# w_in in two tiles, PSUM banks 2 and 2, and both scores of a pair in one visit: an attention and MLP kernel on one core

## The chip, the cores and the metric

The kernel runs on one core of one Trainium2 chip. The metric is the device time of one execution in microseconds (us). Times are medians and ranges of all executions; ratios use fast executions alone (one counts as slow when it is over 1.5% above the fastest of the same kernel). A "span" is the time from the first to the last instruction of the one execution that was profiled, and is 1 to 2 us shorter than that execution's time.

Engines are named as the profile names them: PE is TensorE, PEld its weight loads, DVE VectorE, ACT ScalarE, POOL GpSimd. "Clock" is the share of full speed that was granted to PE.

## The reference

Eight batches of eight heads of attention over 576 positions (four heads with a local mask of 32 positions, four with a strided mask), whose output goes through two layers of an MLP. There are 4608 rows in all; the output is float32.

```python
scores = scale * np.matmul(q, k.transpose(0, 1, 3, 2))        # 8 x 8 heads, 576 x 576, head width 64
masks = [mask_local if h < 4 else mask_strided for h in range(8)]
attn = softmax(where(masks, scores, -1e9))
x = (attn @ v) as 4608 x 512
h = x @ w_in                                                   # 512 x 2048
g = np.where(h > 0.0, h, np.exp(np.minimum(h, 0.0)) - 1.0)
return g @ w_out                                               # 2048 x 512
```

## The kernel before

The masks leave so few positions that attention is cheap. Each batch is handled in eight pieces, four head pairs by two halves: transposes of q and k (T), scores (S), exp on ACT (e), times a 0/1 mask on DVE (pm), then matmuls that give the outputs and their sums (M), and a tail (E): ln and exp on ACT (ln, rc) give the reciprocal of the sums, and DVE multiplies into xT. Layer 1 takes 256 rows of xT and 256 columns of w_in in a group of eight matmuls (hps; a wide form of sixteen is hpw), layer 2 takes quarters of four matmuls into a tile of 128 rows (ops), which ACT copies out (osb).

The results of matmuls land in PSUM. The kernel uses eight banks of it: four for attention and wide groups (two tiles of two banks), three for layer 1, one for layer 2:

```python
p_x = tile_pool(name="ps_x", bufs=2)      # tiles of two banks: scores, wide groups
p_h = tile_pool(name="ps_h", bufs=3)      # layer 1; narrow transposes; s_ps and o_ps of batch 0
p_o = tile_pool(name="ps_o", bufs=1)      # layer 2; at the start, a scratch tile for spins
...
w_in_sb = const([128, KC, d_ff], BF16, "w_in_sb")      # one tile, loaded in two halves
```

Batch 0 is attention alone, with "spins" (matmuls on a constant, whose result nobody reads, f below) put between to keep the clock up:

```python
for it in ("f7 S0 S1 f6 T1 f6 S2 S3 m f10 T2 f6 S4 S5 f3 X3 f3 S6 f3 S7 M4 f3 E4 M5 f3 E5 M6 f3 E6 "
           "v M7 f3 E7 M0 f3 E0 M1 f3 E1 M2 f3 E2 M3 f10 E3").split():
```

T2 is the transposes of pair 2, X3 those of pair 3 (T3q and T3k, in the change, its q and its k apart), p sets the memsets of padding rows, m builds the strided mask, v casts v. The memsets that give constant columns (ones) and zeroed padding rows are on POOL, after this loop:

```python
nc.gpsimd.memset(qs[64:RP], 0.0)          # padding rows, 1.80 us each
nc.gpsimd.memset(ks[64:RP], 0.0)
...
nc.gpsimd.memset(qlb[64:RP], 0.0)
...
for i in range(2):                        # ones beside v: four memsets, 0.74 to 1.23 us each
    for t, n in ((vlx[i], LB), (vsx[i], NS)):
        nc.gpsimd.memset(t...[:, :, 1, :], 1.0)
```

After a second stage (batch 1, first layer-2 tiles) the main loop alternates groups of layer 1 with quarters of layer 2 and starts pieces of attention at set points between them; before the change the two scores of a head pair are half a group apart, so PE goes to attention twice.

The softmax here doesn't subtract the row's maximum and nothing guards it: scores larger than these inputs give would overflow.

## Time and profile before

| | before |
|---|---|
| time, median of 3 | 344.11 us (342.29 to 346.48) |
| span, mean clock | 343.4 us, 0.99 |
| PE, DVE, ACT, POOL busy | 320.0, 241.6, 220.9, 110.3 us |
| last xT of batch 0 ends | 27.37 us |
| first and second matmul of layer 1 | 26.14 and 29.57 us |
| main loop (128 groups of layer 1): start of the fifth, the 107th, the 125th | 81.55, 295.74, 327.00 us |

PE at 93% busy is the bound, and the prediction shows the lines for it. In excerpts in the order of time the columns are start us, us, engine, line, operation, out<-in, shape, count, and in brackets the idle time before it and what ended it.

### The profile page before, as it was taken

The numbers are of one execution on the slowest core, as the hardware profiler recorded it, in microseconds if no ns is written. First come the engines' busy times: TensorE is split into PE (matmuls) and PEld (weight loads), VectorE is DVE, ScalarE is ACT, GpSimd is POOL, SyncE is SP. The second block draws the span as 40 slices with busy tenths as digits, with TensorE's granted clock in tenths as the row PEclk, the third lists the DMA queues.
The fourth block names the chain that finished last, engine by engine and source line by source line (L and its number), as shares of the span: only waits on it lengthen the run. The fifth ranks groups of instructions, "written<-read, shape, count | busy, mean of one in ns | idle before, by whom it ended". The sixth has DMA issues, their size and how long they took to land.

```text
span 343.4 us, 7671 instructions
## 1 busy us (share of the span) xinstructions
PE 320.0 (93%) x2967; PEld 221.7 (65%) x2967; DVE 241.6 (70%) x476; ACT 220.9 (64%) x427; POOL 110.3 (32%) x129
## 2 busy tenths in 40 slices
PE   8686998877999999999999999999999999999995
PEld 6554864456666666676676666666777666777762
DVE  4541994337677788788888887789888776766660
ACT  3483667648667777677787766777777767444441
POOL 8068654830176260727006361545000000000000
PEclk9998999989999999999999999999999999999999
DMA  8999999999269944995169948992191101111211
GB/s 160 185 197 197 222 183 134 122 177 182 43 119 166 201 123 92 158 209 149 31 124 181 201 105 145 208 187 77 43 171 52 32 29 35 32 32 31 52 41 61
DMA packets 55179, 41.98 MB, mean 122 GB/s; under 512 B 38296, under 2 KB 45784, under 8 KB 55144
## 3 DMA queue, kind: packets, MB, share of 16 engines
q0 software_dynamic: 21040, 24.49, 43.5%
q1 hardware_dynamic: 32780, 16.42, 22.7%
q10 hardware_dynamic: 1324, 0.59, 1.0%
q8 instruction: 23, 0.38, 0.5%
q14 instruction: 12, 0.10, 0.1%
HBM read 38.18 MB, written 9.44 MB: 139 GB/s over the span
## 4 chain that ended last, share of the span: by engine, by line
PE 65%; ACT 11%; DMA 10%; DVE 8%; issue 3%; POOL 2%; SPq 0%; ACTq 0%; DVEq 0%
PE ops L451 30%; PE hps L392 27%; DMA w_in_sb<-in_moe_w_in_dram 6%; PE sc L283 3%; ACT osb L456 3%; ACT he L400 2%; DVE g L408 2%; DVE he L407 2%; DMA out_dram<-osb 2%; ACT ln L339 2%; ACT ln L338 2%; PE ox L335 1%; DMA ksT<-ks 1%; DVE g L428 1%; PE tp L258 1%
## 5 line engine op out<-in xcount | busy, mean ns | idle before, releaser
L451 PE MATMUL ops<-w_out_sb,g 128*128 128x512 bf16 x576 | 147.1, 380 | 3.7 <-ACT osb L456 3.5
L392 PE MATMUL hps<-xT,w_in_sb 128*128 128x256 bf16 x1088 | 143.4, 276 | 2.5 <-DVE xT L307 1.8
L392 PEld LDWEIGHTS <-w_in_sb 128*128 128x128 bf16 x1088 | 116.5, 114 | 23.1 <-issue 2.9
L400 ACT ACTIVATE he<-hps 128x512 f32<-128x512 f32 x136 | 80.6, 594 | 63.9 <-PE hps L392 61.8
L408 DVE TENSOR_TENSOR g<-he,hps 128x512 bf16<-128x512 bf16 x130 | 89.3, 687 | 13.9 <-DVE he L407 0.5
L451 PEld LDWEIGHTS <-g 128*128 128x128 bf16 x576 | 52.0, 98 | 44.4 <-issue 5.5
L407 DVE TENSOR_SCALAR he<-he 128x512 bf16<-128x512 f32 x130 | 63.1, 485 | 24.4 <-ACT he L400 23.3
L286 ACT ACTIVATE e<-sc 128x576 bf16<-128x576 f32 (+1 forms) x64 | 40.7, 645 | 14.5 <-PE sc L283 14.5
L456 ACT COPY osb<-ops 128x512 f32<-128x512 f32 x36 | 21.0, 582 | 11.7 <-PE ops L451 11.0
L307 DVE TENSOR_TENSOR xT<-ox,rc 64x288 bf16<-64x288 f32 x40 | 18.2, 454 | 7.3 <-ACT rc L341 6.5
L303 DVE TENSOR_TENSOR xT<-ox,rc 64x288 bf16<-64x288 f32 x40 | 18.1, 454 | 6.3 <-ACT rc L341 5.7
L129 POOL DMA_DIRECT2D qs<-in_q_dram x8 | 6.3, 792 | 39.6 <-DMA qsT<-qs 32.9
L338 ACT ACTIVATE ln<-ox 64x288 f32<-64x288 f32 x40 | 16.3, 407 | 4.1 <-PE ox L335 3.1
L341 ACT ACTIVATE rc<-ln 128x288 f32<-128x288 f32 x40 | 17.8, 444 | 1.3
L288 DVE TENSOR_TENSOR pm<-e,mask_s 72x576 bf16<-72x576 bf16 x32 | 15.2, 492 | 4.2 <-ACT e L286 4.1
L150 POOL COPY vsx<-vs 72x1024 bf16<-72x1024 bf16 x10 | 10.5, 1073 | 21.4 <-DMA vs<-in_v_dram 21.4
L294 DVE TENSOR_TENSOR pm<-e,mask_l 128x576 bf16<-128x576 bf16 x32 | 14.7, 473 | 3.7 <-ACT e L286 3.4
L138 POOL CAST klb<-kl 96x768 bf16<-96x768 f32 x11 | 10.7, 994 | 18.1 <-DMA kl<-in_k_dram 10.7
L144 POOL CAST vlx<-vl 128x768 bf16<-128x768 f32 x13 | 11.2, 889 | 16.1 <-DMA vl<-in_v_dram 13.6
L339 ACT ACTIVATE ln<-ox 64x288 f32<-64x288 f32 x40 | 16.1, 403 | 0.5
L461 PE MATMUL idle<-warm 128*128 128x256 bf16 x83 | 14.4, 315 | 1.3 <-DVE warm L173 1.3
L283 PEld LDWEIGHTS <-ksT 64*128 64x128 bf16 x256 | 5.9, 98 | 11.8 <-issue 7.7
(95 smaller groups left out, 268.8 us busy)
## 6 DMA issues: line engine op xcount, KB each, us to landing
out_dram<-osb SPq DMA_DIRECT2D x32, 144.0 KB
vl<-in_v_dram POOLq DMA_DIRECT2D x7, 576.0 KB, 17.2
kl<-in_k_dram POOLq DMA_DIRECT2D x6, 576.0 KB, 13.9
ql<-in_q_dram POOLq DMA_DIRECT2D x5, 576.0 KB, 14.8
qs<-in_q_dram POOLq DMA_DIRECT2D x8, 288.0 KB, 7.1
ks<-in_k_dram POOLq DMA_DIRECT2D x8, 288.0 KB, 8.8
vs<-in_v_dram POOLq DMA_DIRECT2D x8, 288.0 KB, 9.6
w_in_sb<-in_moe_w_in_dram POOLq DMA_DIRECT2D x2, 1024.0 KB, 19.5
```

The source lines that it names most:

```text
L286: nc.scalar.activation(e[0:R], sc[0:R, :, 0:W], ACT.Exp, scale=scale)
L303: nc.vector.tensor_mul(xs[:, u * W:(u + 1) * W], o[pr], rc[pr])
L307: nc.vector.tensor_mul(dst, o[pr].rearrange(pat, b=3, s=NS), rc[pr].rearrange(pat, b=3, s=NS))
L338: nc.scalar.activation(ln[lo], o[0][hi], ACT.Ln)
L339: nc.scalar.activation(ln[hi], o[1][lo], ACT.Ln)
L341: nc.scalar.activation(rc, ln, ACT.Exp, scale=-1.0)
L392: nc.tensor.matmul(hps[:, mm], lhsT=w_in_sb[:, c, (m // 4) * 512:(m // 4 + 1) * 512].rearrange("c (p mm) -> c mm p", mm=4)[:, m % 4], rhs= ...
L400: nc.scalar.activation(e, hps, ACT.Exp)
L407: eng.tensor_scalar(e1, e, scalar1=1.0, scalar2=1.0, op0=ALU.min, op1=ALU.subtract)
L408: nc.vector.tensor_tensor(gt, e1, hps, op=ALU.max)
L451: nc.tensor.matmul(ops, lhsT=g[:, m, kk * 128:(kk + 1) * 128], rhs=w_out_sb[:, m, :], start=(m == 0), stop=(m == MC - 1))
L456: nc.scalar.copy(o_sb, ops)
```

## The change

Its intent: layer 1's first columns need only the first half of w_in, so two tiles let them start when that half is in; two banks for layer 2 take away its wait for ACT's copy; one visit to the scores instead of two saves PE a switch. To get layer 1 started earlier it also reorders batch 0: the spins write free columns of live banks instead of a bank of their own, a cast moves from ACT to DVE, and the memsets move ahead. The core of the diff:

```diff
-    p_h = ctx.enter_context(tc.tile_pool(name="ps_h", bufs=3, ...))
-    p_o = ctx.enter_context(tc.tile_pool(name="ps_o", bufs=1, ...))
+    p_h = ctx.enter_context(tc.tile_pool(name="ps_h", bufs=2, ...))
+    p_o = ctx.enter_context(tc.tile_pool(name="ps_o", bufs=2, ...))
...
-    w_in_sb = const([128, KC, d_ff], BF16, "w_in_sb")
+    w_in_sb = [const([128, KC, d_ff // 2], BF16, f"w_in_sb{i}") for i in range(2)]
... piece_S: spins from here on go into the scores' bank
+        idle[0] = sc[:, 1, W:512]
... mm_O2, batch 0: s_ps in a layer-2 bank, spins from here on beside it
+            s_ps, idle[0] = ss[:, 0:W], ss[:, W:512]
... the start
-    idle = p_o.tile([128, 256], F32, tag="o", name="idle")
+    first = p_x.tile([128, 256], F32, tag="x", name="idle")
+    idle = [first]
...
+    for i in range(2):
+        for t, n in ((vlx[i], LB), (vsx[i], NS)):
+            nc.gpsimd.memset(t...[:, :, 1, :], 1.0)
-    for it in ("f7 S0 S1 f6 T1 f6 S2 S3 m f10 T2 f6 S4 S5 f3 X3 f3 S6 f3 S7 M4 f3 E4 ...
-               "v M7 f3 E7 M0 f3 E0 M1 f3 E1 M2 f3 E2 M3 f10 E3").split():
+    for it in ("f7 S0 S1 f6 T1 f6 S2 S3 m f8 T2 T3q S4 S5 T3k p f3 S6 S7 M4 f3 E4 ...
+               "v M7 f3 E7 M0 f3 E0 M1 f3 E1 M2 f3 E2 M3 f12 E3").split():
...
+        elif it == "p":
+            for t in (qlb, qs, ks):
+                nc.gpsimd.memset(t[64:RP], 0.0)
         elif it == "v":
-            cast_v(nc.scalar, 0, 0)
+            cast_v(nc.vector, 0, 0)
... (the old memsets after the loop are gone, with them a short one that zeroed rows of vlx)
... (the order of the second stage is new too, and layer 2 now takes all its tiles from p_o)
... second stage: the last narrow group of each tile in a layer-2 bank
-            l1(j, 4 * h + 3)
+            l1(j, 4 * h + 3, bank="o")
... main loop
-                at(SC[b][i] + .5 * u, lambda ...: do(("S", b, p, u)))
+                at(SC[b][i] + (.5 * u if b == 2 else 0), lambda ...: do(("S", b, p, u)))
```

More of the change, by code (lines that the diff above doesn't have):

```diff
@@ L58 @@
     p_x = ctx.enter_context(tc.tile_pool(name="ps_x", bufs=2, space=bass.MemoryType.PSUM))
-    p_h = ctx.enter_context(tc.tile_pool(name="ps_h", bufs=3, space=bass.MemoryType.PSUM))
-    p_o = ctx.enter_context(tc.tile_pool(name="ps_o", bufs=1, space=bass.MemoryType.PSUM))
+    p_h = ctx.enter_context(tc.tile_pool(name="ps_h", bufs=2, space=bass.MemoryType.PSUM))
+    p_o = ctx.enter_context(tc.tile_pool(name="ps_o", bufs=2, space=bass.MemoryType.PSUM))
     ctx.enter_context(tc.manual_schedule())
@@ L191 @@
     for i in range(2):
-        nc.gpsimd.dma_start(out=w_in_sb[:, :, i * 1024:(i + 1) * 1024],
+        nc.gpsimd.dma_start(out=w_in_sb[i],
                             in_=w_in_v[:, :, i * 1024:(i + 1) * 1024])
@@ L248, in piece_T @@
         else:
-            ps = [p_h.tile([128, S], BF16, tag="h", name="tp") for _ in range(2)]
+            ps = [p_h.tile([128, S], BF16, tag="h", name="tp"),
+                  p_o.tile([128, S], BF16, tag="o", name="tp")]
         for i, (dst, blk) in enumerate(both):
@@ L260, in piece_T, with piece_S @@
             copy(engs[i] if engs else nc.vector, dst, ps[i])
-    def piece_S(b, hp, u, fill=0):
+    def piece_S(b, hp, u):
         i_, a, st, pb = b % 2, hp % 2, hp >= 2, pitch(b)
@@ L266, in piece_S @@
         R = RS if st else 128
-        for _ in range(fill):
-            spin(sc[:, 1, W:W + 224])
+        idle[0] = sc[:, 1, W:512]
         for i in range(4 if st else 3):
@@ L350, in mm_O2 @@
         else:
-            s_ps = p_h.tile([128, W], F32, tag="h", name="s_ps")
+            ss = p_o.tile([128, 512], F32, tag="o", name="s_ps") if pool is None else p_h.tile(
+                [128, 512], F32, tag="h", name="s_ps")
             o_ps = p_h.tile([128, W], F32, tag="h", name="o_ps")
+            s_ps, idle[0] = ss[:, 0:W], ss[:, W:512]
         R = RS if hp >= 2 else 128
@@ L381, with w_in_of, l1 @@
     g_of = {}
-    def l1(j, t, mode="A"):
+    def w_in_of(m, c):
+        w = w_in_sb[m // (MC // 2)][:, c].rearrange("c (j p mm) -> c j mm p", mm=4, p=128)
+        return w[:, m // 4 % 2, m % 4]
+    def l1(j, t, mode="A", bank="h"):
         if t == 0:
@@ L386, in l1 @@
         g = g_of[j]
-        hps = p_h.tile([128, 2, SUB], F32, tag="h", name="hps")
+        hps = (p_h if bank == "h" else p_o).tile([128, 2, SUB], F32, tag=bank, name="hps")
         r0 = (j * SUB) % RING
@@ L393, in l1 @@
                     hps[:, mm],
-                    lhsT=w_in_sb[:, c, (m // 4) * 512:(m // 4 + 1) * 512].rearrange(
-                        "c (p mm) -> c mm p", mm=4)[:, m % 4],
+                    lhsT=w_in_of(m, c),
                     rhs=xT[:, c, r0:r0 + SUB],
@@ L419, in l1_wide @@
                     hps[:, mm],
-                    lhsT=w_in_sb[:, c, t * 256:t * 256 + 512].rearrange(
-                        "c (p mm) -> c mm p", mm=4)[:, mm],
+                    lhsT=w_in_of(2 * t + mm, c),
                     rhs=xT[:, c, r0:r0 + SUB],
@@ L482, in do @@
             tail_O2(*it[1:4], mm_O2(*it[1:4], pms.pop(it[1:4]), p_x))
-    idle = p_o.tile([128, 256], F32, tag="o", name="idle")
+    first = p_x.tile([128, 256], F32, tag="x", name="idle")
+    idle = [first]
     def spins(n):
         for _ in range(n):
-            spin(idle)
+            spin(idle[0])
     spins(26)
@@ L498 @@
     P = [(p, u) for p in range(4) for u in range(2)]
-    for it in ("f7 S0 S1 f6 T1 f6 S2 S3 m f10 T2 f6 S4 S5 f3 X3 f3 S6 f3 S7 M4 f3 E4 M5 f3 E5 M6 f3 E6 "
-               "v M7 f3 E7 M0 f3 E0 M1 f3 E1 M2 f3 E2 M3 f10 E3").split():
-        n = int(it[1]) if len(it) > 1 else 0
+    for i in range(2):
+        for t, n in ((vlx[i], LB), (vsx[i], NS)):
+            nc.gpsimd.memset(t.rearrange("p a t (y d) -> p (a t) y d", d=D)[:, :, 1, :], 1.0)
+    for it in ("f7 S0 S1 f6 T1 f6 S2 S3 m f8 T2 T3q S4 S5 T3k p f3 S6 S7 M4 f3 E4 M5 f3 E5 M6 f3 E6 "
+               "v M7 f3 E7 M0 f3 E0 M1 f3 E1 M2 f3 E2 M3 f12 E3").split():
+        n = int(it[1:].strip("qk")) if len(it) > 1 else 0
         if it == "m":
@@ L505 @@
             spins(n)
+        elif it == "p":
+            for t in (qlb, qs, ks):
+                nc.gpsimd.memset(t[64:RP], 0.0)
         elif it == "v":
-            cast_v(nc.scalar, 0, 0)
+            cast_v(nc.vector, 0, 0)
             cast_v(nc.gpsimd, 0, 1)
-        elif it[0] in "TX":
-            piece_T(0, n, (nc.vector, nc.scalar if n > 1 else nc.vector), it[0] == "X")
+        elif it[0] == "T" and len(it) == 3:
+            dst, blk = t_parts(0, n, it[2])
+            pool, tag = (p_h, "h") if it[2] == "q" else (p_o, "o")
+            ps = pool.tile([128, S], BF16, tag=tag, name="tp")
+            for j, x in enumerate(blk):
+                nc.tensor.transpose(ps[:, j * RS:(j + 1) * RS], x, identity[0:RS, 0:RS])
+            copy(nc.vector, dst, ps)
+        elif it[0] == "T":
+            piece_T(0, n, (nc.vector, nc.scalar if n > 1 else nc.vector), False)
         elif it[0] == "S":
@@ L513 @@
         elif it[0] == "M":
-            do(("M", 0, *P[n], p_h))
+            do(("M", 0, *P[n], None))
         else:
@@ L525, in spreads @@
             spread_v(nc.gpsimd, b, a)
-    nc.gpsimd.memset(qs[64:RP], 0.0)
-    nc.gpsimd.memset(ks[64:RP], 0.0)
     load_str(1, qs, q)
@@ L539 @@
     load_wo(3)
-    nc.gpsimd.memset(qlb[64:RP], 0.0)
     load_kl(1, nc.gpsimd)
@@ L543 @@
     load_vl(1, nc.gpsimd)
-    for i in range(2):
-        for t, n in ((vlx[i], LB), (vsx[i], NS)):
-            nc.gpsimd.memset(t.rearrange("p a t (y d) -> p (a t) y d", d=D)[:, :, 1, :], 1.0)
-    nc.gpsimd.memset(vlx[0][0:PRE, :, 0].rearrange("p a (y d) -> p a y d", d=D)[:, :, 0:3:2, :], 0.0)
     for h in range(2):
@@ L568, in l2_to @@
             j, kk, part = L2S[l2n[0]]
-            h = kk and (j == 0 or l2n[0] >= n_late)
-            l2(j, kk, part, *((p_h, "h") if h else (p_o, "o")))
+            l2(j, kk, part, p_o, "o")
             l2n[0] += 1
-    n_late = len(L2S)
-    for it in ("2 S4 2 S5 2 2 X4 2 S6 X5 2 S7 2 X6 2 X7 v "
-               "a 2 T0 2 S0 S1 2 T1 k B0 2 E0 S2 2 B1 S3 E1 2 B2 E2 2 B3 t 2 E3 x").split():
+    for it in ("2 S4 2 S5 2 B4 2 S6 E4 2 A5 S7 E5 2 B6 E6 2 A7 E7 v "
+               "a 2 T0 2 S0 S1 2 T1 k B0 2 E0 S2 2 A1 E1 S3 2 B2 E2 2 A3 t 2 2 E3 x").split():
         n = int(it[-1]) if it[-1].isdigit() else 0
@@ L634 @@
             for u in range(2):
-                at(SC[b][i] + .5 * u, lambda b=b, p=p, u=u: do(("S", b, p, u)))
+                at(SC[b][i] + (.5 * u if b == 2 else 0), lambda b=b, p=p, u=u: do(("S", b, p, u)))
                 at(SC[b][i] + 1.5 + .5 * u,
@@ L646 @@
             f()
-        l1(j, t, mode="B" if n < 18 and n % 3 == 0 else "A")
-    n_late = l2n[0]
+        l1(j, t, mode="B" if n < 18 and n % 3 == 0 else "A",
+           bank="o" if n in (2, 3) else "h")
     l2_to(len(L2S))
```

## The prediction

> **What bounds the kernel now.** I read the page first, then five-microsecond windows, then the order of time at the places where PE stops.
>
> ```profile
> PE 320.0 (93%) x2967; PEld 221.7 (65%) x2967; DVE 241.6 (70%) x476; ACT 220.9 (64%) x427; POOL 110.3 (32%) x129
> ...
> L451 PE MATMUL ops<-w_out_sb,g 128*128 128x512 bf16 x576 | 147.1, 380 | 3.7 <-ACT osb L456 3.5
> L392 PE MATMUL hps<-xT,w_in_sb 128*128 128x256 bf16 x1088 | 143.4, 276 | 2.5 <-DVE xT L307 1.8
> ...
> L400 ACT ACTIVATE he<-hps 128x512 f32<-128x512 f32 x136 | 80.6, 594 | 63.9 <-PE hps L392 61.8
> L408 DVE TENSOR_TENSOR g<-he,hps 128x512 bf16<-128x512 bf16 x130 | 89.3, 687 | 13.9 <-DVE he L407 0.5
> ```
>
> PE is the bound: ACT waits for layer 1 (61.8 us) while PE waits 3.5 us for ACT. Busy time alone does not show PE's pace, so I took the time from one start to the next: an eight-matmul layer-1 group holds PE for 0.88 us, a layer-2 quarter for 0.87. From about 106 us on PE hardly stops. The two soft places are in the start-up (windows: PE, PEld, DVE, ACT and POOL busy, granted clock, DMA):
>
> ```profile
> 30.00:35.00 5.00, 5.00 (x33) 3.94 (x32) 0.60 (x1) 2.57 (x4) 3.56 (x4) 0.66 1.11 212
> ...
> 75.00:80.00 5.00, 4.28 (x43) 3.06 (x43) 2.43 (x5) 3.27 (x6) 0.00 (x0) 0.70 1.03 173
> ```
>
> Both follow an idle PE and run at half clock for 3.5 us. The order of time around the first:
>
> ```profile
> 29.57 2.82 PE L418 MATMUL hpw<-xT,w_in_sb 128*128 128x256 bf16 x15 [3.15 <-DMA w_in_sb<-in_moe_w_in_dram]
> ...
> 34.40 1.22 DVE L428 SCALAR_TENSOR_TENSOR g<-we,wr 128x1024 bf16<-128x1024 f32 x1 [7.03 <-ACT wr L427]
> ...
> 36.67 2.37 DVE L407 TENSOR_SCALAR he<-he 128x512 bf16<-128x512 f32 x1
> ...
> 48.62 1.04 PE L451 MATMUL ops<-w_out_sb,g 128*128 128x512 bf16 x4
> ```
>
> The first matmul of layer 1 went at 26.14, the second waited for w_in to 29.56. The halves were issued at 6.9 and 7.7 us and took 17.2 and 21.8, so they landed at 24.1 and 29.5: the wait is for the half that these columns do not need. The attention of batch 0 gave its last xT at 27.38. From 34.40 to 51.77 DVE is the bound.
>
> **What the Trainium skill says.** "PSUM — Partial Sum Buffer", section "PSUM bank collisions raise a hardware error": two engines may not touch one bank and partition quadrant at once, even in disjoint columns. Here the trace agrees that order is forced: ACT's copy of one half of a transpose tile waits for DVE's copy of the other (2.1 us in two places). "SBUF — State Buffer", "Who interferes with whom": a DVE cast or tensor-scalar in a two-port mode and a GpSimd instruction block each other; the 2.37 us at L407 (0.43 otherwise) lie under four POOL memsets, which agrees. "TensorEngine Tiling (Array Packing)", "Key Properties": a change of tiling mode drains TensorE; below I measure about 0.1 us on each side of a visit to the scores. "TensorE: Matmul & The Clock Gate", "What's actually happening": half clock after an idle window of about 3.4 us. Here idle stretches of 3.3 and 2.0 us gave it, ones of 1.1 to 1.2 did not.
>
> **Part 1, w_in in two tiles, and the new start.** If batch 0 finished as before, layer 1 would start at 27.4 instead of 29.56 and at full clock: 2.1 + about 1.5. But the spinning matmuls now write free columns of a live bank. After scores they wait for the exp; before a logarithm (ln) of the same bank, ln waits for them. In the second half a pair needs: its output matmuls plus three spins 0.7, ln 0.42, rc 0.44, xT 0.51, then the output bank is free for the pair after next: about 2.15 us per two, or 1.08 each, where ACT now sets 0.79. Eight pieces: 8.6 against 8 x 0.79 + 0.81 (the ACT cast that moves to DVE) = 7.1. Twelve spins ahead of the last ln add 0.8. The scores of pieces 6 and 7 start as before (about 18.5), so I get a last xT near 29.2. The memsets of ones now lie at 9 to 12 us, over the k cast of 9.79 us: I add about 1 us. Layer 1 starts at 30.3, not 29.56, but warm (saves 1.5): DVE's first g comes at 30.3 + 1.75 + 2.05 = 34.1. The memsets gone from 36.7 save 1.9 on DVE, so its last g of this stretch ends near 34.1 + 17.4 - 1.9 = 49.6 instead of 51.77.
>
> Against that: the fourth of the narrow layer-1 groups now borrows a layer-2 bank. Layer 2 begins with both row halves of the first tile, so its second quarter (48.62 before) must wait for that last g. PE stands for some 3 us, long enough for half clock: 49.6 + (two quarters and a score, 2.1) + 1.7 = 53.4 for the point that was reached at 52.2 + 0.9 = 53.1. Later a transpose waits for another's copies (+0.75), and a wait for osb of 0.6 goes. The gap before 74.3 us stays: osb, ln, rc and xT still follow the last quarter. Start-up in sum: +0.4.
>
> **Part 2, banks 3 and 1 to 2 and 2.** Every second layer-2 tile waited for ACT's copy of the one before. From 85 to 334 us I summed every hold of PE over 0.12 us (start to start, less the columns' own time) that the trace puts down to osb: 10, in all 4.94 us. These go. But layer 1 now may run only two groups ahead. For each group I set the end of its last DVE read against the start of the group two later; where the read ends later, PE will have to wait. The usual evacuation takes 1.9 us and leaves 0.5 to 1.5. Around attention outputs ACT falls behind:
>
> ```profile
> 214.01 0.45 ACT L341 ACTIVATE rc<-ln 128x288 f32<-128x288 f32 x1
> 214.36 0.56 ACT L456 COPY osb<-ops 128x512 f32<-128x512 f32 x1
> 214.95 0.41 ACT L338 ACTIVATE ln<-ox 64x288 f32<-64x288 f32 x1
> ...
> 216.15 0.58 ACT L400 ACTIVATE he<-hps 128x512 f32<-128x512 f32 x1
> ```
>
> ```profile
> 217.77 0.69 DVE L408 TENSOR_TENSOR g<-he,hps 128x512 bf16<-128x512 bf16 x1
> ```
>
> ```profile
> 213.70 1.04 PE L392 MATMUL hps<-xT,w_in_sb 128*128 128x256 bf16 x8
> 214.97 1.02 PE L451 MATMUL ops<-w_out_sb,g 128*128 128x512 bf16 x4 [0.23 <-ACT osb L456]
> 215.83 1.04 PE L392 MATMUL hps<-xT,w_in_sb 128*128 128x256 bf16 x8
> 216.71 1.03 PE L451 MATMUL ops<-w_out_sb,g 128*128 128x512 bf16 x4
> 217.57 1.04 PE L392 MATMUL hps<-xT,w_in_sb 128*128 128x256 bf16 x8
> ```
>
> The group of 213.70 is read until 218.46; the group two later started at 217.57 (216.30 + 0.87 = 217.17 without the osb hold). It must now start at 218.5: a hold of 1.35 in place of 0.40. The same subtraction, with the lost osb hold and 0.06 for the wake-up added and consecutive overlaps counted once, gives for the four pairs of each batch: batch 3: 1.0, 0.9, 0.9, 1.35; 4: 1.1, 1.3, 0.4, 0.9; 5: 0.15, 1.15, 0.1, 1.35; 6: 1.1, 0.4, 0.05, 0.85; 7: 0.05, 0.85, 0.1, 1.35. Sum 15.4. Net of 4.94: +10.4. After the last output every group leaves 0.55, so the tail is free.
>
> **Part 3, both scores in one visit.** Between 106 and 290 us a visit of eight or six score matmuls costs 0.333 us from start to start, of which 0.10 is entry, 0.11 the matmuls, 0.13 the exit. Two visits cost 0.67, one double visit about 0.46: 0.2 us x 20 pairs = -4.1.
>
> Sum: 344.1 + 0.4 + 10.4 - 4.1 = 350.8. I take 350.0, since whoever made the change probably saw some gain that I miss.
>
> **Rivals.** First, the holds of part 2 come out small, because the scores moved forward relieve ACT and DVE just there. For it: ACT is busy only 64%. Against it: at 214 to 216 the queue holds two tails and an osb and no score. With half the holds: 342 to 343. Second, the spins do not hold ln back and the memsets hit nothing: layer 1 starts near 26.5, warm, 4 to 5 us earlier. For it: the ACT cast really goes. Against it: the bank rule. This makes 346 to 347. Third, the stand before the second layer-2 quarter is worse, with both half-clock stretches: 353 to 355.
>
> **Range and chances.** Start-up is uncertain by 3 us either way, the holds by 4, the visits by 1: together about 5, hence 343 to 356. 2% slower begins at 351.0, just above my centre: 0.42; within 2%: 0.50. Faster by 2% (337.2) needs both the first and the second rival: 0.08.
>
> **What would show it.** Waits of layer 1 (PE hps or its weight load) for DVE g, about 10 to 15 us in all, 0.7 before; waits of ops for osb gone; 20 fewer entries into scores; the first L418 run near 30 us at full clock; a PE gap near 47 to 49 us ended by DVE g, with half clock after it. I am wrong if layer 1 starts before 28 us, or if holds for g stay under 5 us.

## More of the kernel before

```profile
7.48 0.37 DVE L204 COPY mask_l<-base_l 128x576 bf16<-128x576 bf16 x1
...
11.87 0.43 PE L283 MATMUL sc<-qlT,klT 64*128 64x96 bf16 x12 [0.38 <-DVE klT L241]
...
19.65 0.40 ACT L375 ACTIVATE ln<-s_ps 128x288 f32<-128x288 f32 x1
...
26.92 0.46 DVE L307 TENSOR_TENSOR xT<-o_ps,rc 128x288 bf16<-128x288 f32 x1 [0.35 <-ACT rc L377]
```

Four landmarks: a small copy that makes the local mask; the scores of the second head pair; the first ln, with which the eight tails begin; the last xT. Between the first of them and 20.98 us no POOL memset runs.

## The result, and the profile after

| | before | after |
|---|---|---|
| time, median of 3 | 344.11 us | 359.38 us (358.74 to 361.68) |
| ratio of fast runs | | 1.0454 (95% interval 1.0329 to 1.0579) |
| span, mean clock | 343.4, 0.99 | 357.0, 0.956 |
| last xT of batch 0 ends | 27.37 | 37.16 |
| second matmul of layer 1 | 29.57 | 37.22 |
| fifth group of layer 1 in the main loop | 81.55 | 91.15 (+9.6) |
| 107th group | 295.74 | 309.38 (+13.6) |
| 125th group | 327.00 | 340.64 (+13.6) |

A ratio, here and below, is the mean time of one kernel's fast runs over that of the other's of the same rounds, so not quite the ratio of the medians.

It is slower by 15 us, 9 more than predicted and outside my range. The offsets between the two traces place it: 9.6 us are lost before the main loop's fifth group, 4.0 us between the fifth and the 107th, nothing after. (That is 13.6 and not 15.3, because the profiled execution of before took 345.22 us, 1.1 over its median, and that of after 358.74, 0.6 under its own. Offsets taken against before's trace, here and below, may flatter the other kernel by that 1.1.) I had written +0.4 for the first of these and 10.4 - 4.1 = 6.3 for the second.

**The main loop** looks as predicted. Two of the costliest groups of the page (busy us, mean ns of one, then idle time before them and what ended most of it):

```profile
L398 PE MATMUL hps<-xT,w_in_sb 128*128 128x256 bf16 x1088 | 140.8, 273 | 14.2 <-DVE g L413 12.3
L455 PE MATMUL ops<-w_out_sb,g 128*128 128x512 bf16 x576 | 149.4, 384 | 3.3 <-DVE g L413 3.3
```

Layer 1 now waits 12.3 us for g (0.7 before; the 1.8 for xT are there both times), and layer 2 no longer waits for osb (3.5 before). Its 3.3 for g are one wait in the start, shown below. Counted from one start to the next, as in the prediction, 15 holds for g cost 14.8 us.

**The start** doesn't. The four landmarks again, with what lies between the first two:

```profile
7.47 4.38 DVE L204 COPY mask_l<-base_l 128x576 bf16<-128x576 bf16 x1
...
8.44 0.79 POOL L506 MEMSET vlx<- 128x768 bf16 x1
...
9.64 0.73 PE L465 MATMUL sc<-warm 128*128 128x224 bf16 x6 [1.16 <-ACT e L286]
...
10.68 1.00 POOL L506 MEMSET vsx<- 72x1024 bf16 x1
...
12.64 0.66 PE L259 MATMUL tp<-identity,qlb 72*128 72x72 bf16 x8 [2.27 <-DVE qlb L135]
...
14.83 0.66 PE L283 MATMUL sc<-qlT,klT 64*128 64x96 bf16 x12
...
24.43 0.41 ACT L377 ACTIVATE ln<-s_ps 128x288 f32<-128x288 f32 x1 [0.35 <-PE s_ps L465]
...
36.70 0.46 DVE L307 TENSOR_TENSOR xT<-o_ps,rc 128x288 bf16<-128x288 f32 x1 [2.52 <-ACT rc L379]
```

The mask copy takes 4.38 us instead of 0.37: it ends with the last of the four memsets of ones, which the change moved here. The cast of q behind it is late, PE waits 2.27 us for it, having just waited 1.16 us for an exp (the spins, meant to fill such gaps, now write the bank that this exp reads). From there the first ln comes 4.8 us late, and from the first ln to the last xT it takes 12.7 us where it took 7.7.

Why the second stretch is longer, the windows show (PE, PEld, DVE, ACT, POOL busy with counts, clock, DMA share, GB/s):

```profile
8.34:11.75 3.41, 0.87 (x14) 0.57 (x6) 3.41 (x1) 1.19 (x2) 3.35 (x5) 1.00 1.34 196
...
21.99:25.40 3.41, 3.27 (x44) 2.02 (x42) 1.66 (x5) 2.04 (x4) 3.35 (x4) 0.50 1.09 205
...
32.23:35.64 3.41, 3.41 (x24) 2.45 (x23) 0.92 (x2) 1.02 (x3) 1.51 (x2) 0.50 1.08 206
```

In the window that ends at 11.75 PE was busy for a quarter. From 11.75 to 35.64 its clock is 0.50, although the records show it 70 to 100% busy all that time. These edges are those of the recorded clock, and they are regular: every stretch at half clock, in every trace of this case that I read, lasts a whole number of 3.41 us (apart from those that the kernel's end cuts). The Trainium skill states this step, in "TensorE: Matmul & The Clock Gate", section "What's actually happening": the clock is decided in windows of 4096 cycles, 3413 ns, that run freely and aren't reset by a kernel's start. The traces agree:

| trace | stretches at half clock (us), in windows of 3.41 |
|---|---|
| before | 30.23 to 33.64 (1), 74.60 to 78.01 (1) |
| after | 11.75 to 35.64 (7), 56.12 to 62.95 (2) |

The second stretch of after follows the wait that I had predicted, the second layer-2 quarter for the last g of the start:

```profile
56.16 0.69 DVE L413 TENSOR_TENSOR g<-he,hps 128x512 bf16<-128x512 bf16 x1
56.90 1.86 PE L455 MATMUL ops<-w_out_sb,g 128*128 128x512 bf16 x4 [3.33 <-DVE g L413]
```

### The profile page after: what moved, and what is told of

Its sections match the earlier page's. It is cut to its first block, busy times and chain, and to the rows that moved or that the text cites.

```text
span 357.0 us, 7676 instructions
## 1 busy us (share of the span) xinstructions
PE 321.9 (90%) x2973; PEld 226.9 (64%) x2973; DVE 248.1 (70%) x478; ACT 217.2 (61%) x425; POOL 108.4 (30%) x128
## 4 chain that ended last, share of the span: by engine, by line
PE 59%; DVE 17%; ACT 14%; DMA 5%; issue 4%; DVEq 0%; ACTq 0%; SPq 0%
PE ops L455 25%; PE hps L398 23%; DVE g L413 5%; DVE he L412 4%; ACT he L405 4%; PE sc L283 3%; ACT ln L339 2%; ACT ln L338 2%; DMA out_dram<-osb 2%; PE s_ps L465 2%; ACT osb L460 2%; DVE xT L303 2%; PE tp L259 1%; DVE g L432 1%; ACT rc L341 1%
## 5 line engine op out<-in xcount | busy, mean ns | idle before, releaser
L398 PE MATMUL hps<-xT,w_in_sb 128*128 128x256 bf16 x1088 | 140.8, 273 | 14.2 <-DVE g L413 12.3
L455 PE MATMUL ops<-w_out_sb,g 128*128 128x512 bf16 x576 | 149.4, 384 | 3.3 <-DVE g L413 3.3
L455 PEld LDWEIGHTS <-g 128*128 128x128 bf16 x576 | 53.4, 98 | 42.7 <-issue 5.0
L412 DVE TENSOR_SCALAR he<-he 128x512 bf16<-128x512 f32 x130 | 61.6, 474 | 25.2 <-ACT he L405 23.8
L286 ACT ACTIVATE e<-sc 128x576 bf16<-128x576 f32 (+1 forms) x64 | 38.5, 646 | 23.0 <-PE sc L283 23.0
L460 ACT COPY osb<-ops 128x512 f32<-128x512 f32 x36 | 21.0, 583 | 13.6 <-PE ops L455 13.0
L288 DVE TENSOR_TENSOR pm<-e,mask_s 72x576 bf16<-72x576 bf16 x32 | 15.5, 514 | 9.1 <-ACT e L286 9.0
L294 DVE TENSOR_TENSOR pm<-e,mask_l 128x576 bf16<-128x576 bf16 x32 | 15.3, 501 | 3.7 <-ACT e L286 3.2
L138 POOL CAST klb<-kl 96x768 bf16<-96x768 f32 x11 | 10.2, 942 | 17.9 <-DMA kl<-in_k_dram 10.4
L465 PEld LDWEIGHTS <-warm 128*128 128x128 bf16 x89 | 10.4, 127 | 7.3 <-issue 2.7
L129 POOL DMA_DIRECT2D vs<-in_v_dram x8 | 5.7, 714 | 24.6 <-PE so L370 23.3
```

What stands on the lines that cost most here:

```text
L286: nc.scalar.activation(e[0:R], sc[0:R, :, 0:W], ACT.Exp, scale=scale)
L398: nc.tensor.matmul(hps[:, mm], lhsT=w_in_of(m, c), rhs=xT[:, c, r0:r0 + SUB], start=(c == 0), stop=(c == KC - 1))
L412: eng.tensor_scalar(e1, e, scalar1=1.0, scalar2=1.0, op0=ALU.min, op1=ALU.subtract)
L455: nc.tensor.matmul(ops, lhsT=g[:, m, kk * 128:(kk + 1) * 128], rhs=w_out_sb[:, m, :], start=(m == 0), stop=(m == MC - 1))
L460: nc.scalar.copy(o_sb, ops)
```

## The experiments

**Theories.** Mine: in the start, the early memsets and the spins in live banks let PE stand between 8 and 13 us, which brings the half clock, and the half clock stretches the rest; the layer-2 bank adds the hold at 53 to 57 us; in the main loop the two banks of layer 1 cost the holds for g. Rivals: the spins' hold on ln alone is the cost (as I had predicted its mechanism); or w_in's early start and the rest of the reorder are worth something that the banks hide; or the half clock only follows and costs nothing. Four sets were run, all with correct results, each beside runs of the kernel before on one chip: e1 to e4, e5 to e8, e9 to e12, e13 to e15. The before of these sets had medians of 343.71, 343.24, 343.71 and 343.68 us.

### Parts of the change alone

**e1: the kernel before with w_in in two tiles, nothing else.**

```diff
-    w_in_sb = const([128, KC, d_ff], BF16, "w_in_sb")
+    w_in_sb = [const([128, KC, d_ff // 2], BF16, f"w_in_sb{i}") for i in range(2)]
```

> The kernel before with w_in in two tiles and nothing else. My theory: the second layer-1 matmul starts at about 27.5 us instead of 29.56, PE idles 1.3 us instead of 3.3, so no half clock follows, and the DVE-bound stretch starts some 3.5 us earlier: about 340.7 us, ratio near 0.99. Rival (the wait is hidden anyway: DVE, the later loads or the memsets on POOL take it back before 74 us): 343.5 to 344.5.

Measured: 342.21 us (20 runs), ratio 0.9989 (0.9960 to 1.0018): no gain that can be told from none. In its trace the wait for w_in is gone and the fifth group of the main loop starts at 78.12 (81.55 before), but k landed late in that run (its cast starts at 11.53 us, 9.79 in before), a window at half clock followed from 13.54, and the last xT came at 29.30. The interval leaves room for a gain of some 1.4 us; the 3.4 us that I had hoped for lie outside it.

**e2: the kernel before with the merged visits, nothing else.**

```diff
-                at(SC[b][i] + .5 * u, lambda ...: do(("S", b, p, u)))
+                at(SC[b][i] + (.5 * u if b == 2 else 0), lambda ...: do(("S", b, p, u)))
```

> The kernel before with both scores of a pair in one visit from batch 3, nothing else. Theory: 20 entries into scores fewer, 0.2 us each, no new holds for DVE g: 339.5 to 340 us. Rival (the two exps in a row put ACT behind, so part of the layer-1 holds of the changed kernel come from this and not from the banks): 344 or more, with holds of hps on DVE g of a few us.

Measured: 340.88 us (15 runs), ratio 0.9899 (0.9864 to 0.9934), which is 3.5 us off the before of its rounds. The theory holds, if a little short of its 339.5 to 340: the merged visits gain about what I had given them (4.1). No wait for g comes with it; those for osb stay (4.0 us).

### Parts of the change undone

**e3: after, with the four memsets of ones back in their old place** (the first four lines removed at the start and put back after the loads of v).

```diff
-    for i in range(2):
-        for t, n in ((vlx[i], LB), (vsx[i], NS)):
-            nc.gpsimd.memset(t...[:, :, 1, :], 1.0)
... after load_vl(1, nc.gpsimd)
+    (the same three lines)
```

> The changed kernel with the four memsets of ones put back to where they were on POOL. Theory (memsets and spins each hold up the start): the mask copy takes 0.4 us instead of 4.38, the second pair's scores start near 12 us instead of 14.8, and with PE's gaps then at 1.3 us the clock stays full; layer 1 starts near 30 us instead of 35.5, 352 to 354 us in all. Rival (the held spins alone let the clock drop): the mask copy is short but the clock falls to half all the same before 20 us, layer 1 starts at 32 to 34 us, 356 to 358 us. Rival (the memsets cost nothing): 359.

**e4: after, with the spins in a bank of their own until the layer-2 tiles need it.**

```diff
-    first = p_x.tile([128, 256], F32, tag="x", name="idle")
+    first = p_o.tile([128, 256], F32, tag="o", name="idle")
-        idle[0] = sc[:, 1, W:512]
+        idle[0] = first[:, 0:224]
-            s_ps, idle[0] = ss[:, 0:W], ss[:, W:512]
+            s_ps = ss[:, 0:W]
```

> The changed kernel with the spins in a layer-2 bank of their own during batch 0 (s_ps then has one bank), memsets left early. Theory: the mask copy stays at 4.4 us and T1 late (12.6 us), so one half-clock stretch may come, but the free spins bring the clock back within 3.5 us; ACT paces the pairs of outputs at 0.8 us instead of 1.3; layer 1 starts at 31 to 32 us: 354 to 356 us. Rival (the bank rule does not matter, the slow clock comes from the late mask alone): the clock stays at half to 30 us or more and the time within 1.5 us of 359.

Measured: e3 355.26 us, ratio 1.0357 (1.0274 to 1.0440); e4 351.80 us, ratio 1.0275 (1.0218 to 1.0332). Landmarks of the start, with what they say:

| | before | after | e3 | e4 |
|---|---|---|---|---|
| mask copy, us | 0.37 | 4.38 | 0.38 | 4.38 |
| first ln | 19.65 | 24.43 | 20.74 | 22.66 |
| last xT ends | 27.37 | 37.16 | 32.25 | 31.77 |
| at half clock before 36 us, in windows | 1 | 7 | 3 | 4 (in two parts) |

With the memsets back the mask copy is short again, so they are what held it: shown. Each of the two edits brings the last xT some 5 us forward, and neither brings it back to 27.4. e3 came out above its theory's range and below its rival's, and in part the rival is right: the clock falls all the same, at 18.60 us. The spins still wait for exps there (1.16 us at 9.93 and at 14.13), and memsets of padding rows lie over the last window before the fall. e4 came out below its range. Its clock falls at 11.52 us although its spins are free, because PE stands 3.47 us for the late cast of q; so the early memsets are enough to bring the first fall. But full clock is back at 18.34 (it is lost once more from 21.76 to 28.58), and not at 35.64.

**e5: both of these edits.**

```diff
-    for i in range(2): ... nc.gpsimd.memset(t...[:, :, 1, :], 1.0)      # and back after load_vl, as e3
-            s_ps, idle[0] = ss[:, 0:W], ss[:, W:512]                    # spins apart, as e4
+            s_ps = ss[:, 0:W]
```

> The changed kernel with both the memsets put back and the spins in a bank of their own. Theory: the two losses of the start add up (4.1 and 7.6 us in the two runs before), layer 1 starts near 28 us at full clock, and the kernel takes 346 to 349 us; what is left over the kernel before is the stand before the second layer-2 quarter (about 5 us) and the holds for DVE g less the visits. Rival (each alone already saves the same half clock): no better than 351.

Measured: 353.94 us (349.82 to 355.03), ratio 1.0255 (1.0176 to 1.0334). Missed: the two don't add, and the rival's "no better than 351" holds. In the profiled run PE stood 2.39 us for the cast of k, and five windows at half clock followed, 12.71 to 29.78; last xT 31.40. I took k to have landed late and didn't know what else let the clock fall. The trace says otherwise:

```profile
9.58 1.80 POOL L513 MEMSET qlb<- 16x2048 bf16 x1 [0.69 <-PE tp L259]
10.05 1.75 DVE L138 CAST klb<-kl 96x768 bf16<-96x768 f32 x1 [1.46 <-DMA kl<-in_k_dram]
```

k was there at 10.05, 0.26 us later than in before, and its cast took 1.75 us instead of 0.56, under a memset of padding rows that the change had moved ahead as well. (In e8, below, k did land late: its cast starts at 11.21 and takes 0.56.)

**e6: after, with the last narrow group of the second round in a layer-1 bank.**

```diff
-            l1(j, 4 * h + 3, bank="o")
+            l1(j, 4 * h + 3, bank="h" if h else "o")
```

> The changed kernel, but in the second half of the first two tiles the fourth narrow layer-1 group takes a layer-1 bank again, so that layer 2 finds both of its banks free. Theory: the 3.3 us wait of ops for DVE g goes and with it the 5.8 us of half clock after it: 354 to 356 us. Rival (DVE is the bound there, its last g comes when it comes, and the wait only moves to the next pair of outputs): the half clock stays or the time is within 1.5 us of 359.

Measured: 354.21 us, ratio 1.0286 (1.0218 to 1.0354). The second quarter goes 1.19 us after the first (4.60 in after), no half clock follows, and the main loop's first scores come 4.6 us earlier (the second matmul of its first layer-1 group at 80.45, 85.08 in after). The predicted hold was real and is the bank's.

**e7: after, with layers 1 and 2 drawing on one pool of four banks.**

```diff
-    p_h = ctx.enter_context(tc.tile_pool(name="ps_h", bufs=2, ...))
-    p_o = ctx.enter_context(tc.tile_pool(name="ps_o", bufs=2, ...))
+    p_h = ctx.enter_context(tc.tile_pool(name="ps_h", bufs=4, ...))
+    p_o = p_h                              # and one tag, "h", throughout
```

> The changed kernel with its four single banks in one pool that both layers draw from, merged visits kept. Theory (two banks for layer 1 are too few): the holds of hps for DVE g from 100 us on (14.8 us) go nearly all, the holds for osb do not come back, and the wait of the second layer-2 quarter goes too, while the slow start stays: 339 to 342 us. Rival (ACT is behind by itself, the merged visits included): holds for g stay over 7 us, time over 348.

Measured: 342.78 us (20 runs), a little over the theory's 339 to 342; ratio 0.9981 (0.9958 to 1.0004), against 1.0454 for the change as it stands. Its page, the first of the same two groups:

```profile
L398 PE MATMUL hps<-xT,w_in_sb 128*128 128x256 bf16 x1088 | 140.9, 273 | 1.8 <-DVE xT L307 1.8
```

The wait for g is gone, and none for osb has come back (layer 2: 0.0 idle). Batch 0 is as slow as in after (last xT 37.3). The second layer-2 quarter no longer waits, and the fifth group starts 2.9 us earlier than in after (88.24). Most of the gain is in the main loop: from the fifth group to the 107th it takes 205.5 us, against 214.2 before and 218.2 after. The holds were a matter of how four banks were dealt out, not of their number.

**e8: all three: memsets of ones back, spins apart, one pool.**

```diff
-    for i in range(2): ... nc.gpsimd.memset(t...[:, :, 1, :], 1.0)      # and back after load_vl, as e3
-            s_ps, idle[0] = ss[:, 0:W], ss[:, W:512]                    # spins apart, as e4
+            s_ps = ss[:, 0:W]
-    p_o = ctx.enter_context(tc.tile_pool(name="ps_o", bufs=2, ...))     # one pool, as e7
+    p_o = p_h
```

> The changed kernel with memsets back, spins apart and one pool of four banks. Theory: start mended (11 us) and main loop mended (15 us and 5 us): 331 to 334 us, faster than the kernel before by 3%. Rival (the mends overlap): 336 to 340.

Measured: 338.44 us (338.03 to 339.52), ratio 0.9832 (0.9785 to 0.9879): faster than before (whether by 2% the interval doesn't say), and in the rival's range, not the theory's. Six windows at half clock remain, five of them from 11.15 to 28.22 us.

### What still holds the start

**e9: e5 with more spins while k lands.**

```diff
-    for it in ("f7 S0 S1 f6 T1 f6 ...
+    for it in ("f7 S0 S1 f33 T1 f6 ...
```

> e5_both_mended with 33 spin matmuls ahead of the first transposes of q instead of 6, so that TensorE stays busy while k lands. Theory (the half clock of the first 30 us is what makes the start late, and it comes from TensorE's idle waits near 9 to 12 us): no half clock from about 14 us on, the last xT of batch 0 near 29, layer 1 from about 29 (31.2 in e5), some 2 to 3 us under e5: 350 to 352. Rival (the half clock is a follower, the start is late by VectorE's and GpSimd's work): clock better, yet last xT at 31 as before, 353 to 354.

Measured: 354.48 us, ratio 1.0283 (1.0219 to 1.0346). The clock stays full until 18.62, not throughout as the theory had it, and last xT is at 31.21: the rival's number. But the trace names what I had missed:

```profile
15.09 1.80 POOL L513 MEMSET qs<- 16x2048 bf16 x1 [1.15 <-PE tp L522]
15.10 1.83 DVE L214 TENSOR_SCALAR eq<-same 72x72 bf16<-72x72 int32 x1
...
17.62 0.44 PE L283 MATMUL sc<-qsT,ksT 64*128 64x72 bf16 x16 [2.60 <-DVE qsT L241]
```

One of the other memsets that the change moved ahead, of the padding rows, lies exactly over a DVE operation that takes 0.19 us otherwise (14.04 us in before). PE waits 2.60 us behind it, in the window from 15.2 to 18.6 it is busy for 29%, and the half clock comes at 18.62.

The same trace bears on the rival of the spins. At half clock the tails keep this pace, first in after, where ln waits for the spins, then in e9, where it doesn't:

```profile
24.33 0.45 PE L360 MATMUL s_ps<-pm,ones 72*64 72x288 bf16 x2
...
25.62 0.45 PE L360 MATMUL s_ps<-pm,ones 72*64 72x288 bf16 x2
```

```profile
23.36 0.45 PE L360 MATMUL s_ps<-pm,ones 72*64 72x288 bf16 x2
...
24.65 0.45 PE L360 MATMUL s_ps<-pm,ones 72*64 72x288 bf16 x2
```

1.29 us from pair to pair in both; before, at full clock, the seven steps from the first of these rows to the eighth took 6.72 us, 0.96 each. So within the row of tails, at half clock, the hold on ln costs nothing: PE itself, with three spins a pair, sets the pace. What the hold would cost at full clock no run shows, since each run that has it passes this row at half clock. Here only the last ln pays, since twelve spins lie ahead of it:

```profile
ACT ln L377 <- PE s_ps L465: 5.5, 8, 2.1
```

(waits: us in total, times, longest). 2.1 of the 5.5 us are that one.

**e13: e5 with the padding memsets back in their old places too.**

```diff
-    ... "T3k p f3 S6 S7 M4 ...
+    ... "T3k f3 S6 S7 M4 ...
... after the loop, before the loads of qs and ks
+    nc.gpsimd.memset(qs[64:RP], 0.0)
+    nc.gpsimd.memset(ks[64:RP], 0.0)
... before load_kl(1, nc.gpsimd)
+    nc.gpsimd.memset(qlb[64:RP], 0.0)
```

> e5_both_mended with the memsets of the padding rows of qlb, qs and ks back in their old places (after the last xT of batch 0), so that no GpSimd memset is left in the first 20 us. Theory (the early memsets hold VectorE up, TensorE then waits, and the half clock follows): the mask constant eq takes 0.19 us and not 1.83, scores of piece 6 near 18.5, half clock in the first 30 us at most 7 us (unless k lands late), last xT of batch 0 28 to 29.5, total 349 to 351. Rival (the half clock comes from the order of scores and transposes, with or without memsets): half clock over 10 us before 30 us again, last xT over 30.5, 353 to 355 as e5 and e9.

Measured: 350.18 us (349.21 to 353.32), ratio 1.0204 (1.0137 to 1.0271), within the theory's range.

```profile
14.15 0.19 DVE L214 TENSOR_SCALAR eq<-same 72x72 bf16<-72x72 int32 x1
...
17.47 0.66 PE L283 MATMUL sc<-qsT,ksT 64*128 64x72 bf16 x16 [1.35 <-DVE ksT L241]
```

The mask constant is short again, the scores of piece 6 go at 17.47 (18.02 before), the first ln at 19.02 (19.65 before): the first 19 us cost nothing any more. The last xT ends at 29.63 (27.37 before). What stays is half clock, three windows from 17.50 to 27.74, after a window in which PE was busy for a third: it waits twice, 0.96 and 1.35 us, for copies of the new order's transposes, which are both on DVE now. Here the rival is partly right: it had over 10 us of half clock, which come to 10.24, where the theory allowed 7. The row of tails begins 0.87 us earlier than before (18.06 against 18.93) and its seven steps take 9.85 us instead of 6.72, which makes the 2.26 that the last xT is late. Six of the steps are 1.20 to 1.41 us, the pace of half clock; one of 2.07 waits for the cast of v, moved to DVE and once more under a memset (1.75 us, that of ks at 22.09).

### Versions that beat both

**e10: the kernel before with w_in in two tiles, merged visits and one pool of four banks** (the edits of e1, e2 and e7; the start and its memsets as before).

```diff
-    w_in_sb = const([128, KC, d_ff], BF16, "w_in_sb")                   # as e1
+    w_in_sb = [const([128, KC, d_ff // 2], BF16, f"w_in_sb{i}") for i in range(2)]
-                at(SC[b][i] + .5 * u, ...)                               # as e2
+                at(SC[b][i] + (.5 * u if b == 2 else 0), ...)
-    p_o = ctx.enter_context(tc.tile_pool(name="ps_o", bufs=1, ...))     # as e7
+    p_o = p_h                                                           # p_h: bufs=4
```

> The kernel before with w_in in two tiles, merged visits and one pool of four banks for both layers; its old start-up order kept. Theory (visits -3.5, osb holds -4.9, no holds for g, start as before): 344 - 3.5 - 5 = 334 to 336. Rival (the savings overlap): 337 to 339.

Measured: 332.94 us (331.20 to 333.68), ratio 0.9651 (0.9587 to 0.9716), a little better than expected.

**e11: e10 with the memsets of ones moved to about 70 us, and the last tail of batch 1 ahead of the last layer-2 quarter.** (In the order below, B stands for the matmuls that give a piece's outputs and sums, E for its tail, 2 for a quarter of layer 2, t for batch 2's transposes, x for loads.)

```diff
-               "... B2 E2 2 B3 t 2 E3 x").split():
+               "... B2 E2 2 B3 E3 t 2 x").split():
... at step x
+            (the three lines of the memsets of ones; the short one of zeros in vlx is dropped)
```

> e10 with the memsets of ones moved to about 70 us and the tail of the last pair of the first stage ahead of the last layer-2 quarter, so that TensorE doesn't stand 2.0 us before the main loop's first scores and doesn't run at half clock after it (4 us at half clock, so 2 us). Theory: 3 to 4 us under e10, 330 to 332. Rival (the gap only moves): within 1 us of e10.

Measured: 334.24 us (333.00 to 335.88), ratio 0.9699 (0.9633 to 0.9765): no gain over e10. The memsets had only found another victim:

```profile
72.54 1.00 POOL L599 MEMSET vsx<- 72x1024 bf16 x1
72.73 2.67 DVE L410 TENSOR_SCALAR he<-he 128x512 bf16<-128x512 f32 x1
...
76.61 0.45 PE L358 MATMUL so<-pm,ones 72*64 72x288 bf16 x2 [3.41 <-DVE pm L288]
```

PE waits 3.41 us for work behind that DVE operation, and two windows at half clock follow, 75.02 to 81.84. In this profiled run two more lie in the start, 20.40 to 27.23, though nothing in e11's first 36 us differs from e10; e14 makes use of that.

**e14: e10 with only the tail moved; the memsets stay at 36 us.**

```diff
-               "... B2 E2 2 B3 t 2 E3 x").split():
+               "... B2 E2 2 B3 E3 t 2 x").split():
```

> e10 with only the tail of the last pair ahead of the last layer-2 quarter; the memsets of ones stay in their old place (36 us). Theory (e11's loss was the memsets over VectorE's tensor-scalar at 72.7, not the tail): a VectorE group there of 0.42 us each, no wait of 3.4 us for pm near 73, no half clock after 74; 330 to 332. Rival (the tail itself brings the wait): as e11, 334.

Measured: 331.65 us (329.82 to 332.92), ratio 0.9645 (0.9588 to 0.9701). The same operation without the memsets:

```profile
72.80 0.42 DVE L410 TENSOR_SCALAR he<-he 128x512 bf16<-128x512 f32 x1
```

PE's wait there is 1.16 us and no half clock follows. So the memsets, not the tail, made e11's wait, as the theory had it. Whether the tail's move gains anything against e10 can't be told: the intervals cover each other.

The two traces also say what half clock costs by itself. Up to 36 us e11 and e14 run the same instructions, and their first ln come at 19.56 and 19.46. Then e11 has its two windows at half clock, and its seven steps from the first row of sums to the eighth take 8.70 us; in e14, at full clock, they take 6.72. So two windows cost this row 2.0 us: here the half clock doesn't only follow a delay, it makes one.

**e15: e14 with the memsets of ones on DVE, while it waits for the first q.**

```diff
+    for i in range(2):
+        for t, n in ((vlx[i], LB), (vsx[i], NS)):
+            nc.vector.memset(t...[:, :, 1, :], 1.0)
     spins(26)
     cast_q(nc.vector, 0)
-    (the three lines on POOL, and the short memset of zeros in vlx)
```

> e14 with the four memsets of ones done by VectorE while it waits for the first q (idle until 5.3 us). Theory (a memset on GpSimd costs VectorE's stretch 2 us at 36.7 in the kernel before): the tensor-scalar near 35 takes 0.43 us, last g of the start 1.5 to 2 us earlier, 328 to 330.5. Rival (VectorE's memsets delay the first cast, or layer 1 waits elsewhere): 330 to 333, within 1 us of e14.

Measured: 331.77 us (329.57 to 333.00), ratio 0.9653 (0.9580 to 0.9725): as e14. The DVE operation near 35 us takes 0.44 us (2.37 in before), which is what the theory wanted; but in the profiled run three windows at half clock came from 17.64 on, and the last xT was at 30.10 instead of e14's 27.18. Up to the scores of piece 6 the two traces show the same order at nearly the same times. They differ in where the clock's windows lie, and in the last one before the fall PE was busy for 56% here. So the start of the old order stands near the edge too, and the gain of the memsets isn't separated from that.

**e12: after with spins apart, one pool, memsets of ones late, and the tail ahead.**

```diff
-            s_ps, idle[0] = ss[:, 0:W], ss[:, W:512]                    # as e4
+            s_ps = ss[:, 0:W]
-    p_o = ctx.enter_context(tc.tile_pool(name="ps_o", bufs=2, ...))     # as e7
+    p_o = p_h
-    (the three lines of the memsets of ones at the start)               # to step x, as e11
-               "... B2 E2 2 A3 t 2 2 E3 x").split():
+               "... B2 E2 2 A3 E3 t 2 2 x").split():
```

> The kernel after with spins in two banks of their own, one pool of four banks, the memsets of ones late, and the tail of the last pair ahead of the last layer-2 quarter. Theory (e8 gave 338.4 with the half clock in the first 28 us): 334 to 337, still over e11 by the half clock of the start. Rival (without memsets near the start the clock recovers early): 330 to 332, level with e11.

Measured: 332.89 us (332.51 to 333.57), ratio 0.9658 (0.9587 to 0.9729), between both expectations, and level with e10. In the profiled run four windows at half clock came in the start, 13.79 to 27.45: k's cast met the memset of qlb's padding rows and took 1.20 us instead of 0.56.

All of e10, e12, e14 and e15 are some 3.5% faster than the kernel before and, by the ratios, some 7.7% faster than the change as it was (0.965 over 1.045); they can't be told apart. So the new start, with most of its holds mended (e12), is worth nothing that shows against the old one (e10), and no more is w_in in two tiles by itself (e1). One kernel, e14, stands here as the better version of both.

## Why the prediction was wrong

Its likeliest class (within 2%) and its range were wrong: the measured 359.38 us lie 9.4 over its number and 3.4 over its range. By its own steps:

1. **"Start-up in sum: +0.4" failed; it was +9.6.** Its term "Layer 1 starts at 30.3, not 29.56, but warm" carries most of it: the second matmul of layer 1 went at 37.22, 6.9 us later, and after seven windows of half clock. I had seen that the memsets would lie over a cast of DVE and added "about 1 us". I didn't ask what else DVE does there: the mask copy takes 0.37 us in before, and with four memsets back to back beside it took 4.38. The half clock I had put only where before showed it. I hadn't looked at how near PE was to losing the clock in the first 15 us of before, where it is busy for 58% of the window from 9.7 to 13.2 us.

2. **That ln waits for the spins, at 1.08 us a pair, didn't set the pace.** The pace was 1.29 at half clock, with or without the hold (e9); I had reckoned with a warm PE, and that case no run shows. (The sum has two slips, too: its terms 0.7, 0.42, 0.44 and 0.51 make 2.07 and not 2.15, and 27.38 with the 1.5 of 8.6 less 7.1 and the 0.8 added is 29.7, not 29.2. Neither matters beside 6.9.) Spins do cost here, in two other ways: they can't fill PE's wait for an exp of their own bank (1.16 us at 9.64), and at half clock they take PE's own time. The "twelve spins ahead of the last ln", 0.8, were right in kind; at half clock they took 2.42 us.

3. **The memsets gone from 36.7: right.** From the first g to the twelfth it takes 15.8 us (17.4 before, 15.5 predicted).

4. **"PE stands for some 3 us" before the second layer-2 quarter, "long enough for half clock": right, but undersized.** 3.33 us, then two windows at half clock and not one. PE was busy for 77 and 100% of them, and half of that busy time, 3.0 us, is my estimate of what they cost: 1.3 more than the 1.7 I gave. e6 shows that the bank is the cause. Of the 9.2 us that I was off in the start, 6.9 are in layer 1's start, 1.3 here, 1.0 I haven't traced.

5. **Part 2: right.** Holds for g: 15.4 predicted, 14.8 measured; e7 takes them away by dealing the banks differently, and nothing else.

6. **Part 3: right.** 4.1 predicted; e2 gives 3.5. The sum of the main loop was 6.3 predicted and is 4.0 in the traces. Summed from start to start between the fifth group and the 107th, the two traces differ by +14.8 for g, -4.4 for osb, -4.4 at the entries to scores and the exits, and -2.0 in small changes, of which a wait for pm (0.6) is the largest. These 2.0 the prediction didn't have.

The third rival of the prediction (353 to 355, worse stands and half clock) pointed the right way, but for the layer-2 quarter only. What the early memsets do in the start is shown by e3 (mask copy) and e13 (the first 19 us), that half clock by itself delays the tails by e11 and e14. How much of the loss is delay of DVE and how much half clock can't be cut cleanly, because each makes the other: from before to after, 4.8 us are lost up to the first ln and 5.0 from there to the last xT. For the latter, the seven steps from the first row of sums to the eighth take 9.68 us (23.03 to 32.71) instead of 6.72, which is 3.0, and the last ln's wait is 2.1.

## What to carry to other kernels

Before moving a memset or a copy on GpSimd, list every short operation of VectorE in the stretch it will lie over, and who waits for those: a stretch of free time on GpSimd isn't free for VectorE (0.37 us became 4.38 here). Where the clock depends on PE's activity, look at PE's busy share in pieces of 3.4 us of the kernel before. In these traces, leaving out their last microsecond, the falls came after windows with 14 to 71% of PE busy, and no window with more was followed by one; so treat a place near half busy as one microsecond away from several windows at half speed, and don't look for a sharp limit. And before splitting banks between two users by number, ask whether one pool serves both: here it removed the waits of either split.

## What the Trainium skill lacked or had wrong

- "TensorE: Matmul & The Clock Gate", section "What's actually happening", gives about 3.4 us of sustained activity for the return to full clock. In after, windows with 74, 70, 80, 96, 96 and 93% of PE's records busy didn't bring it back and only one of 100% did (0.50 from 11.75 to 35.64 us); in e15, too, it took three windows near 100%. In before one window of 100% was enough, in e2 one of 85% (28.97 to 32.38). Those in after and e15 were rows of short matmuls, those in before and e2 mostly longer ones; what is counted as activity these runs don't settle.
- The same section gives the fall after an idle window. Here it needs no idle window: windows with 25% (after), 33% (e13), 44% (e10) and 46% (before, 71.19 to 74.60) of PE busy brought it. It isn't a sharp share of these records either: one of 46% in e9 (76.6 to 80.0 us) didn't, one of 56% in e15 and one of 71% in e11 (16.99 to 20.40) did.
- "SBUF — State Buffer", section "Who interferes with whom", says that whoever issues first gets the shared ports for that instruction, and the other blocks. The traces agree on the blocking, but by the records the order of issue didn't decide: a DVE copy recorded from 7.47 us lost to all four memsets that followed one another from 8.44 to 11.68 (4.38 us in place of 0.37), and a tensor-scalar to three (2.67 in place of 0.42, e11). The starts of POOL's records are rough, so only the length of the wait is sure. The page doesn't say that back-to-back GpSimd instructions can keep DVE out that long.
- "TensorEngine Tiling (Array Packing)", section "Key Properties", says that a change of mode drains TensorE, without a figure: a visit to the scores costs 0.10 us on the way in and 0.13 on the way out in before, and merging twenty pairs of visits gained 3.5 us (e2).
